# A planned order with other step lengths, one check instruction per unit pair, and a third PSUM bank for VectorE

## The chip, the core and the metric

The kernel runs on one core of a Trainium2 chip. The metric is the device time of one execution in microseconds. Five engines work side by side and meet through semaphores only: TensorE (PE) multiplies into PSUM, which has eight banks of 512 float32 per partition; ScalarE (ACT) and VectorE (DVE) read PSUM; GpSimd (POOL) works on SBUF; SyncE (SP) issues most DMAs. Each engine takes its own instructions strictly in the order in which they were written.

## The reference

Two branches over the same input `x` (2048 tokens of 512) are mixed by a gate.

```python
g = _sigmoid((x * gate_w).sum(-1, keepdims=True))
# A: 32 heads of 16, one shared key and value head
q = (x @ wq).reshape(B, S, H, Dh).transpose(0, 2, 1, 3)
k = x @ wk
v = x @ wv
scores = einsum('bhqd,bkd->bhqk', q, k) * Dh ** (-0.5)
p = softmax(scores, axis=-1)
a = einsum('bhqk,bkd->bhqd', p, v) ... @ wo
# B: gated MLP with a 2048 x 2048 mixing over tokens
z = gelu(einsum('bsd,df->bsf', x, w_in))
z1 = z[..., :Fh]
z2 = layernorm(z[..., Fh:])
g2 = einsum('ts,bsf->btf', w_sp, z2) + b_sp[None, :, None]
b = einsum('bsf,fd->bsd', z1 * g2, w_out)
return g * a + (1 - g) * b
```

The largest part is the exponential of the scores: 32 heads x 2048 queries x 2048 keys.

## The kernel before

**Blocks and units.** The scores are cut into blocks of 128 keys x 512 queries for one head. A unit is 512 queries and four heads, with 16 key tiles: 64 blocks. There are 32 units, so 2048 blocks. For each block PE forms scores (tile `ps` from `KA` and `QA`, "S" below), another engine forms the exponential, and PE multiplies it with the values ("PV").

**Two engines form the exponential.** ScalarE evaluates it directly for most blocks, two or three PSUM banks per instruction ("step", `exp_op`, L825), and writes tile `P`, a ring of `PB` slots of 512 columns. VectorE approximates it for the others by a polynomial of degree four: it reads the PSUM bank with a scale and an offset (`d_A`, L837, one bank or two neighbouring banks in one instruction), squares the result (`d_u`, L845) and squares it again (`d_w`, L851), all in tile `UW`. POOL can do part of the second squaring (also L851), in quarters of 256 columns; a block is two quarters. What the polynomial lacks in lower orders is added by small matmuls with `KTV` and `SVB`. VectorE gets its blocks in batches of four (one key tile, four heads); a batch reserves a slot of `UW`. No batch is fixed to an engine in advance: the planner opens a new batch when a VectorE bank comes free.

**Banks.** ScalarE's steps alternate between banks 0 and 1 and banks 2, 3 and 4 (`EB`). VectorE has bank 5 and may take bank 4 (`DBK`); when it does, ScalarE's step has two blocks in place of three. One bank collects PV (`BO`) and one serves all other matmuls (`BM`, the fill bank): projections, the gated MLP, the token mixing, the output rows. Those come as groups of matmuls that hold the bank from the first matmul until VectorE has read it. Where PE would be idle for too long, it gets a group of matmuls on zeros (tag "warm").

**The planner.** The order on every engine is written out before the launch by a discrete simulation inside the kernel file. Whichever engine has the earliest free time takes its next step (`pe_step`, `act_step`, `dve_step`, `pool_step`), with lengths from constants: one ScalarE step of n blocks keeps the engine for `426.7 * n + A_OV` ns (`act_period`); one VectorE read takes 601 ns and each further bank 533 ns; a square takes 65 ns plus 0.52 ns per column; a POOL square of n quarters takes `C_P0 + C_P1 * n`, 184 + 428 n. `C_SW` is the cost of changing between S and other matmuls on PE, `L_PE` and `L_X` the delays from one engine to another, `D_END` and `D_DEP` those behind a VectorE instruction. The hardware runs the resulting order; the constants matter there only through that order and through how many blocks went to each engine.

**Rules of the planner.** `hungry(now)` estimates VectorE's outstanding work, 600 ns for every PSUM bank that waits for it among it. Bank 4 goes to VectorE while `hungry` is below `FLEX`. A unit gives VectorE no more batches when fewer than `RMIN` (in the last unit `RLAST`) blocks would be left. `pool_try` starts POOL's work only for as long as VectorE is expected to read PSUM (`psum_work`), with a tolerance `PSL`: a POOL square of n quarters is issued if the coming reads last at least `C_P0 + C_P1 * n - PSL`.

**Checks and normalisation.** At the end of a unit VectorE transposes the PV bank to `T1`. After every second unit VectorE takes reciprocals (`rc`), POOL multiplies them with the gate (`rr`, L881) and applies them (`Tn`, L891). The polynomial is only good for bounded scores, so 16 units carry a check: POOL compares two columns of `T1` with a threshold (L916) and multiplies the outcome into `good` (L917). Two VectorE instructions reduce `good` to a flag near the end (`bad_ops`, L921 and L922); a flag other than zero would make all engines run a slow exact path.

Of the kernel before, what the change touches and what calls it, by code (L numbers as in the profile page):

```python
# [20 lines left out]
NST = 16  # L21
NU = 32
LN_EPS = 1e-5
PB = 24
ND = 6
NQ = 3
NMAX = 8
# [18 lines left out]
N0 = 3  # L46
A_OV = 63.3
HEAD = 45000.0
C_TN = 1250.0
C_T2 = 7000.0  # L50
# [120 lines left out]
def build_kernel(nc, x_d, wq_d, wk_d, wv_d, wo_d, win_d, wsp_d, bsp_d, wout_d, gw_d, out_d):  # L171
    es = ExitStack()
    with es:
# [62 lines left out]
        good = sb("good", [128, 16, 2], F32)  # L236
        gtmp = sb("gtmp", [128, 16, 2], F32)
# [28 lines left out]
        op("dve", lambda v: v.memset(good[:], 1.0), w=["good"])  # L266
# [136 lines left out]
        C_MM, C_V, C_344, C_SW, C_256, C_1ST = 216.0, 216.0, 146.0, 103.0, 110.0, 10.0  # L403
        L_PE, L_X = 250.0, 60.0
        D_END, D_DEP = 85.0, 117.0
        C_DA, C_TT, C_EV = 601.0, 1130.0, 600.0

        T = {}
# [502 lines left out]
            return lambda: pgx.op("dve", lambda v: v.transpose(OT.rearrange("p r b (g i) -> p r (b g i)", i=32)[:, c % 2, 512 * jp:512 * jp + 512], Tn[:, pr, :]),  # L911
                                  r=[("Tn", pr, 0, 0), ("Tn", pr, 1, 0)], w=[("OT", c % 2, jp)], tag="T2")

        def good_op(jj):
            def f():
                op("pool", lambda v: v.tensor_scalar(gtmp[:], t1v[:, jj, :, 17:19], thr[:, 0:1], None, ALU.is_le), r=[("T1", jj, 0), "thr"], w=["gtmp"], tag="good")  # L916
                op("pool", lambda v: v.tensor_tensor(good[:], good[:], gtmp[:], ALU.mult), r=["gtmp", "good"], w=["good"], tag="good")  # L917
            return f

        def bad_ops():  # L920
            op("dve", lambda v: v.tensor_reduce(goodp[:], good[:], AX.XY, ALU.min), r=["good"], w=["goodp"], tag="bad")  # L921
# [4 lines left out]
        def unit_end(u, t):  # L926
            c, j = u // 8, u % 8
            jj, jp = j % 2, j // 2
            pr = jp % 2
            if u == NU - 1:  # L930
                for h in range(2):
                    dq(t1_q, 370.0, t1_op(pg, u, 256 * h, 256 * h + 256), t, None)
                no = [norm_ops(pg, c, jp, [1], 8 * h, 8 * h + 8, [("T1", 1, 256 * h)]) for h in range(2)]
                for z in range(len(no[0])):
                    for h in range(2):
                        dq(t1_q, *no[h][z], t, None)
                for h in range(2):
                    rk = [("Tn", pr, 0, 0), ("Tn", pr, 1, 8 * h)]
                    dq(t1_q, 370.0, t2_op(pg, c, jp, 256 * h, 256 * h + 256, rk, ("OT", 3, 3, h)), t, setT(("OT", 3, 3, h)))
                return  # L940
            tf = t1_op(pg, u)

            def t1f():
                assert u < 2 or (u - 2) in t1_done, u
                tf()
            dq(t1_q, 625.0, t1f, t if u < 2 else (lambda: max(t, T.get(("TnE", (u - 2) // 2), 1e12))), setT(("O", u)))
            if chk_of(u) is not None:
                dq(pl_q, 390.0, good_op(jj), (lambda: when(("k2", 3), ("O", u))), None)
            if u == NU - 2:
                for c_, f_ in norm_ops(pg, c, jp, [0]):  # L950
                    dq(norm_q, c_, f_, (lambda: when("RT", ("O", u))), None)
                return
            if jj == 1:
                no = norm_ops(pg, c, jp, [0, 1], eng="pool", big=True)
                dq(norm_q, no[0][0], no[0][1], (lambda: when("RT", ("O", u))), setT(("rc", u)))
                dq(pl_q, 200.0, no[1][1], (lambda: when(("rc", u))), setT(("rr", u)))

                def tn():
                    no[2][1]()
                    t1_done.update((u - 1, u))  # L960
                def tne(t):
                    T[("TnE", u // 2)] = t
                    if jp == (2 if c == 3 else 3):
                        t2_dma(c, t)
                dq(pl_q, C_TN, tn, (lambda: when(("rr", u))), tne)
            if u == NU - 3:
                dq(norm_q, 250.0, bad_ops, (lambda: when(("TnE", u // 2))), setT("bad"))

        T["wqd0"] = 6400.0
        T["wqd"] = 17000.0  # L970
# [120 lines left out]
        def d_busy(b):  # L1091
            return b in slots and slots[b]["cur"] is not None

        def d_bank(now, flex=True):
            for b in DBK:
                d = dbs[b]
                if b < 5 and not flex:
                    continue
                if d["k"] is not None and (d["k"] not in eend or eend[d["k"]] + L_X > now):
                    continue  # L1100
                if d["blk"] is None and not d_busy(b) and max(d["free"], slots[b]["free"] if b in slots else 0.0) <= now:
                    return b
            return None
# [7 lines left out]
        def d_soon(now):  # L1111
            if d_busy(DBK[0]) or not (db["todo"] or new_batch(now)):
                return None
            t = []
            f = free["dve"]
            for b in DBK:
                if b < 5 and len(DBK) > 1:
# [118 lines left out]
        def add_checks(now):  # L1236
# [20 lines left out]
            if pu < NU and pu not in chk_added:  # L1257
# [3 lines left out]
                elif ("QS", q) in T:  # L1261
                    chk_added.add(pu)
                    for g in range(4):
# [2 lines left out]
                            T[("QSfree", q)] = clk["now"] + 300.0  # L1266
                        add_item(pu, g, (T[("QS", q)], f, None, None))

        def fill_pick(now):
            for b in slots:  # L1270
                s = slots[b]
                g = s["cur"]
                if g is not None and g.pos < len(g.pieces):
                    p = g.pieces[g.pos]
                    r = 0.0 if len(p) < 3 else p[2]()
                    if r is not None and r <= now:
                        return s, g, None
            cand = []
            if first:
                cand.append(first)  # L1280
            else:
                cand.append(early)
            if qs and 2 * qs[0][0] <= st_["ua"] + 3:
                cand.append(qs)
            cand += [outs, main, tails]
            for src in cand:
                if not src:
                    continue
                g = src[0][1] if src is qs else src[0]
                s = slots[g.bank]  # L1290
                if s["cur"] is not None or s["free"] > now:
                    continue
                r = g.ready()
                if r is not None and r <= now:
                    return s, g, src
            return None
# [21 lines left out]
        def pe_step(now):  # L1318
            r = pe_work(now)
            if r is None:  # L1320
# [8 lines left out]
                elif now > W_HEAD and b < (1.0 if now < 20000.0 else W_GEL if gst["arm"] and gst["t"] > now - 8000.0 else pr["W_MIN"]) * W_WIN:  # L1329
# [3 lines left out]
                    if (topen is None or t_end + 40.0 <= lim) and (ds is None or ds > t_end):  # L1333
                        zb = None
                        if (u < NU and all((u, g) in started for g in range(4)) and all(x < unit_total(u) // 4 for x in pv_g[u])
                                and slots[BO]["cur"] is None and slots[BO]["free"] <= now):
                            zb = BO
                        elif slots[BM]["cur"] is None and slots[BM]["free"] <= now:
# [331 lines left out]
        def pool_try(now, rem=0.0):  # L1670
# [27 lines left out]
            for m in sorted(pq):  # L1698
                hd, ud, wb, th, tu, pw = pq[m]
                i = 8 - pw  # L1700
                n = min(nh, i - wb)
                if n <= 0 or (i - 1) // 4 >= ud or tu + 80.0 > now:
                    continue
                d_w("pool", m, i - n, i, after=pg.ops["dve"][-2:-1])
                c_ = C_P0 + C_P1 * n
                plc["lock"] = now + c_
                plc["free"] = now + c_ + 60.0
                w_add(m, i - n, i, now + c_ + 100.0 + L_X)
                pq[m][5] = pw + n
                w_end(m)  # L1710
                return
# [14 lines left out]
        def dve_step(now):  # L1726
# [15 lines left out]
            rd = sorted((d["ord"], b) for b, d in dbs.items() if d["blk"] is not None and d["ready"] <= now)  # L1742
            if len(rd) == 1 and pr["HOLD"] and now > HEAD and st_["ua"] < NU - 1 and not gst["on"]:
                b = rd[0][1]
                o = dbs[DBK[1] if b == DBK[0] else DBK[0]]
# [257 lines left out]
```

## Time and profile before

| | us |
|---|---|
| median of 3 runs | 723.12 (723.04 to 724.63) |
| profiled execution | 723.15 |
| its span, first to last instruction | 721.3 |
| ScalarE busy | 704.6 |
| VectorE busy | 702.4 |
| PE busy | 700.9 |
| POOL busy | 519.7 |

The span is what the trace covers; 1.85 us of the profiled execution's time lie around it. PE's busy time says little about a limit, since its matmuls overlap and their ends are modelled. A row of a group of instructions gives the busy time of the group and the mean length of one, and a length includes the overlap with the instruction before it on the same engine, so lengths may add up to more than the engine's busy time.

### The profile page before, as it was taken

How to read it: one execution, taken by the hardware profiler on the slowest of the kernel's cores; microseconds unless marked ns; L12 is line 12 of the kernel's file. 1: busy time of each engine (PE TensorE's matmuls, PEld its weight loads, DVE VectorE, ACT ScalarE, POOL GpSimd, SP SyncE). 2: the span in 40 equal slices, each digit the busy share in tenths (PEclk: the TensorE clock that was granted, in tenths of full speed). 3: DMA queues.
4: the chain of work that ended last, by engine and by line, in shares of the span. 5: the costliest groups of instructions: out<-in, count | busy, mean ns of one | idle time of the engine just before them, and what ended most of it. 6: DMA issues, size and time to landing. Idle time of an engine off the chain costs nothing. (4 is left out here: it accounts for less than half of the span.)

```text
span 721.3 us, 20958 instructions
## 1 busy us (share of the span) xinstructions
PE 700.9 (97%) x8572; PEld 204.6 (28%) x8572; DVE 702.4 (97%) x1014; ACT 704.6 (98%) x759; POOL 519.7 (72%) x469
## 2 busy tenths in 40 slices
PE   8999999999999999999999999999999999999896
PEld 3322232234222232222223222222322222222222
DVE  5999999999999999999999999999999999999996
ACT  5999999999999999999999999999999999999995
POOL 5468778774467778787677877768877777777772
PEclk9999999999999999999999999999999999999999
DMA  8453000000001015000002410000150000000101
GB/s 162 130 99 64 2 1 2 2 2 3 2 1 31 2 30 97 24 1 2 1 2 39 102 39 9 2 2 1 31 90 16 16 16 17 1 2 2 31 2 34
DMA packets 59808, 20.07 MB, mean 28 GB/s; under 512 B 54805, under 2 KB 59193, under 8 KB 59705
## 3 DMA queue, kind: packets, MB, share of 16 engines
q1 hardware_dynamic: 57448, 18.36, 12.1%
q8 instruction: 69, 1.13, 0.7%
q10 hardware_dynamic: 2256, 0.30, 0.3%
q14 instruction: 35, 0.28, 0.1%
HBM read 3.38 MB, written 2.10 MB: 8 GB/s over the span
## 5 line engine op out<-in xcount | busy, mean ns | idle before, releaser
L825 ACT ACTIVATE P<-ps 128x1024 bf16<-128x1024 f32 (+1 forms) x739 | 679.4, 1211 | 1.8 <-PE ps L387 1.5
L851 POOL TENSOR_TENSOR UW<-UW 128x512 f16<-128x512 f16 (+2 forms) x331 | 426.6, 1289 | 144.0 <-DVE UW L851 59.8
L837 DVE TENSOR_SCALAR UW<-ps 128x512 f16<-128x512 f32 (+1 forms) x418 | 356.4, 874 | 3.2 <-PE ps L387 1.8
L387 PE MATMUL ps<-QA,KA 32*128 32x512 bf16 x2048 | 322.1, 384 | 11.6 <-ACT P L825 6.8
L387 PE MATMUL ps<-P,V 128*32 128x512 bf16 x1480 | 186.9, 386 | 0.2 <-DVE KN L558 0.2
L845 DVE TENSOR_TENSOR UW<-UW 128x2048 f16<-128x2048 f16 (+1 forms) x176 | 182.3, 1036 | 1.3
L387 PEld LDWEIGHTS ps<-QA,KA 32*128 32x128 bf16 x2048 | 88.8, 91 | 312.5 <-ACT P L825 162.9
L387 PE MATMUL ps<-wT,z 128*32 128x512 bf16 (+1 forms) x1536 | 113.4, 366 | 0.0
L387 PE MATMUL ps<-UW,V 128*32 128x512 f16 x568 | 109.6, 385 | 0.2
L851 DVE TENSOR_TENSOR UW<-UW 128x1024 f16<-128x1024 f16 (+5 forms) x161 | 99.4, 629 | 0.0
L387 PEld LDWEIGHTS ps<-P,V 128*32 128x32 bf16 x1480 | 42.6, 94 | 59.9 <-issue 57.6
L387 PEld LDWEIGHTS ps<-wT,z 128*32 128x32 bf16 x1536 | 26.4, 94 | 42.5 <-issue 42.2
L387 PE MATMUL ps<-wout,z 128*32 128x512 bf16 x384 | 32.5, 384 | 0.0
L534 POOL TENSOR_TENSOR QSQ<-QA 128x512 bf16<-128x512 bf16 x16 | 23.8, 1490 | 10.9 <-DVE QA L530 4.1
L387 PEld LDWEIGHTS ps<-UW,V 128*32 128x32 bf16 x568 | 25.4, 94 | 20.0 <-issue 14.8
L387 PE MATMUL ps<-win,xT 128*32 128x344 bf16 x512 | 30.3, 312 | 0.7 <-DVE z L641 0.4
L863 DVE STREAM_TRANSPOSE T<-ps 128x512 f32<-128x512 f32 (+1 forms) x33 | 22.8, 694 | 2.1 <-PE ps L387 2.1
L387 PE MATMUL ps<-CT,zer 128*32 128x512 bf16 x256 | 23.2, 382 | 0.0
L387 PE MATMUL ps<-CT,SVB 128*32 128x512 bf16 x128 | 22.8, 383 | 0.0
L387 PE MATMUL ps<-xT,win 128*32 128x512 bf16 (+1 forms) x384 | 22.3, 363 | 0.2 <-ACT P L825 0.2
L387 PE MATMUL ps<-QA,KTV 128*32 128x512 bf16 x128 | 22.3, 385 | 0.0
L387 PE MATMUL ps<-xT,wqd 128*32 128x512 bf16 x256 | 21.1, 384 | 0.3 <-DMA xT<-in_A_x_dram 0.2
(113 smaller groups left out, 326.1 us busy)
## 6 DMA issues: line engine op xcount, KB each, us to landing
out_dram<-outsb SPq DMA_DIRECT2D x15, 128.0 KB, 2.6
win<-in_B_w_in_dram SPq DMA_DIRECT2D x1, 1376.0 KB, 8.0
wout<-in_B_w_out_dram SPq DMA_DIRECT2D x1, 640.0 KB, 4.6
wo<-in_A_wo_dram SPq DMA_DIRECT2D x8, 64.0 KB, 2.3
KA<-KA SPq DMA_DIRECT2D x4, 112.0 KB, 2.4
UW<-in_A_wq_dram SPq DMA_DIRECT2D x1, 384.0 KB, 4.0
wT<-in_B_w_sp_dram SPq DMA_TRANSPOSE x16, 4.5
UW<-in_A_wq_dram ACTq DMA_DIRECT2D x1, 128.0 KB, 4.1
```

What stands on the lines that cost most here:

```text
L387: return t.matmul(dst, lhsT, rhs, start=start, stop=stop, tile_position=tp)
L534: dq(pl_q, 1050.0, lambda: op("pool", lambda v: v.tensor_tensor(QSQ[:, q % 2, :], QA[:, q % NQ, :], QA[:, q % NQ, :], ALU.mult), r=[("Q", ...
L825: op("act", lambda a: a.activation(P[:, 512 * p0:512 * (p0 + n)], ps[:, 512 * b0:512 * (b0 + n)], ACT.Exp), r=[bkey(b0 + i_) for i_ in ran ...
L837: op("dve", lambda v: v.tensor_scalar(UW[:, s, 512 * i:512 * (i + n)], bank(b, 512 * n), Q_A, Q_AS, ALU.mult, ALU.add), r=[bkey(b + j) for ...
L845: op("dve", lambda v: v.tensor_tensor(src, src, src, ALU.mult), r=k, w=k, tag="dTT")
L851: op(eng, lambda v: v.tensor_tensor(src, src, src, ALU.mult), r=[("U", s, h) for h in range(a // 2, (b + 1) // 2)], w=w, after=after, tag= ...
L863: return lambda: pgx.op("dve", lambda v: v.transpose(T1[:, jj, c0:c1], bank(BO, c1 - c0, c0)), r=[bkey(BO)], w=[("T1", jj, c0)], tag="T1")
```

## The change

It changes the planner's constants and some of its rules, the check, and which banks VectorE may use. The work of the reference, its matmuls and its DMAs stay as they are; the order of all of them is planned anew.

- VectorE's banks are 5, 6 and 4. The fill bank is bank 6 now (it was 7) and the PV bank is 7. VectorE gets bank 6 only when no fill group holds it, when `hungry` is below `BMH` and when the fill work is not behind a straight line that ends at `TFE` (`lag`). Fill groups wait while VectorE has the bank.
- A check is one POOL instruction that writes a slot of its own in `good`; the multiplication into a common tile and the memset of it go. The reduction at the end covers 512 columns in place of 32.
- The ring `P` has 26 slots in place of 24.
- The lengths that the planner assumes: `A_OV` 63.3 to 50, `C_SW` 103 to 98, `L_X` 60 to 40, `D_DEP` 117 to 105; a check 390 to 370, `rr` 200 to 260, the reduction 250 to 750; the normalisation of the last but one unit now counts POOL's hold of the port. Quarters that POOL squares count as ready 400 ns later (`PMG`).
- Thresholds: `RLAST` 12 to 20, `RMIN` 36 to 44, `FLEX` 5000 to 3500, `D_HG` 2800 to 2600, `PSL` 80 to 0, `TTR` 0 to 50 and others.

```diff
-PB = 24
+PB = 26
-DBK = (5, 4)
-BKO = 6
+DBK = (5, 6, 4)
+SHB = 4
+BKO = 7
-RLAST = 12
+RLAST = 20
-A_OV = 63.3
+A_OV = 50
-PR = dict(HALF=100.0, IDR=10, IDN=4, WRES=16, D_HG=2800.0, D_FL=False, WIN=1000.0, WIH=560.0, BACK=32, PRESS=5, FLEX=5000.0, RMIN=36, WBL=0.5, W_MIN=0.8, TTR=0.0, PMX=3, WMX=1000.0, PTO=6000.0, PSL=80.0, WP0=45000.0, WG=0, HOLD=0.0, RLEND=0)
+PR = dict(HALF=50.0, IDR=11, IDN=4, WRES=18, D_HG=2600.0, D_FL=False, WIN=1000.0, WIH=560.0, BACK=34, PRESS=5, FLEX=3500.0, RMIN=44, WBL=0.4, W_MIN=0.78, TTR=50.0, PMX=3, WMX=1000.0, PTO=6000.0, PSL=0.0, WP0=45000.0, WG=0, HOLD=0.0, RLEND=0, BMH=2400.0, FST=0.0, TFE=760000.0, PMG=400.0)
+NCHK = 16
+L_PE = 250
+L_X = 40
+D_END = 85
+D_DEP = 105
+C_SW = 98
...
-        def good_op(jj):
-            def f():
-                op("pool", lambda v: v.tensor_scalar(gtmp[:], t1v[:, jj, :, 17:19], thr[:, 0:1], None, ALU.is_le), r=[("T1", jj, 0), "thr"], w=["gtmp"], tag="good")
-                op("pool", lambda v: v.tensor_tensor(good[:], good[:], gtmp[:], ALU.mult), r=["gtmp", "good"], w=["good"], tag="good")
-            return f
+        def good_op(jj, i):
+            return lambda: op("pool", lambda v: v.tensor_scalar(good[:, i, :, :], t1v[:, jj, :, 17:19], thr[:, 0:1], None, ALU.is_le),
+                              r=[("T1", jj, 0), "thr"], w=[("good", i)], tag="good")
...
+        def d_bm(now):
+            if now < HEAD or hungry(now) >= pr["BMH"] or gst["arm"] and (gel or gst["on"]):
+                return False
+            return not lag(now)
...
+        def lag(now):
+            if gst["arm"] and (gel or gst["on"]):
+                return True
+            n = sum(len(g.pieces) for q in (early, main, outs) for g in q)
+            if ft["n"] is None:
+                ft["n"] = n
+                ft["t"] = now
+            return n > ft["n"] * (pr["TFE"] - now) / (pr["TFE"] - ft["t"])
...
-                if b < 5 and not flex:
+                if b == SHB and not flex or b == BM and not d_bm(now):
...
-                if s["cur"] is not None or s["free"] > now:
+                if s["cur"] is not None or s["free"] > now or g.bank in dbs and (dbs[g.bank]["blk"] is not None or dbs[g.bank]["free"] > now):
...
-                w_add(m, i - n, i, now + c_ + 100.0 + L_X)
+                w_add(m, i - n, i, now + c_ + 100.0 + L_X + pr["PMG"])
```

More of the change, by code (lines that the diff above doesn't have):

```diff
@@ L235, in build_kernel @@
         thr = sb("thr", [128, 1], F32)
-        good = sb("good", [128, 16, 2], F32)
-        gtmp = sb("gtmp", [128, 16, 2], F32)
+        good = sb("good", [128, NCHK, 16, 2], B16)
         goodp = sb("goodp", [128, 1], F32)
@@ L401, in build_kernel @@
             mm(bank(0), CT[:, 0:128], CT[:], True, True, ["CT"], [bkey(0)], tag="warm")
-        C_MM, C_V, C_344, C_SW, C_256, C_1ST = 216.0, 216.0, 146.0, 103.0, 110.0, 10.0
-        L_PE, L_X = 250.0, 60.0
-        D_END, D_DEP = 85.0, 117.0
+        C_MM, C_V, C_344, C_256, C_1ST = 216.0, 216.0, 146.0, 110.0, 10.0
         C_DA, C_TT, C_EV = 601.0, 1130.0, 600.0
@@ L966, in unit_end @@
             if u == NU - 3:
-                dq(norm_q, 250.0, bad_ops, (lambda: when(("TnE", u // 2))), setT("bad"))
+                dq(norm_q, 750.0, bad_ops, (lambda: when(("TnE", u // 2))), setT("bad"))
         T["wqd0"] = 6400.0
@@ L1116, in d_soon @@
             for b in DBK:
-                if b < 5 and len(DBK) > 1:
+                if b in (SHB, BM):
                     continue
@@ L1290, in fill_pick @@
                 s = slots[g.bank]
-                if s["cur"] is not None or s["free"] > now:
+                if s["cur"] is not None or s["free"] > now or g.bank in dbs and (dbs[g.bank]["blk"] is not None or dbs[g.bank]["free"] > now):
+                    continue
+                if g.bank == BM and now > HEAD and not first and src is not qs and hungry(now) < pr["FST"] and not lag(now):
                     continue
@@ L1337, in pe_step @@
                             zb = BO
-                        elif slots[BM]["cur"] is None and slots[BM]["free"] <= now:
+                        elif slots[BM]["cur"] is None and slots[BM]["free"] <= now and dbs[BM]["blk"] is None and dbs[BM]["free"] <= now:
                             zb = BM
```

14 lines of the change are left out of this document (7 added, 7 removed).

## The prediction

> **What bounds the kernel now.** I read the page first (span, busy times), then the busy time by stretches of the span, cut where ScalarE's first and last exponentials and its gelu stage stand, then the groups of instructions with shapes kept apart.
>
> ```profile
> span 721.3 us, 20958 instructions
> PE 700.9 (97%) x8572; PEld 204.6 (28%) x8572; DVE 702.4 (97%) x1014; ACT 704.6 (98%) x759; POOL 519.7 (72%) x469
> ...
> core 0: us, PE busy (x) PEld busy (x) DVE busy (x) ACT busy (x) POOL busy (x), PEclk, DMA share, GB/s
> 0.00:9.01 9.01, 7.34 (x111) 3.19 (x115) 4.31 (x15) 1.56 (x2) 5.00 (x24) 1.00 0.90 164
> 9.01:155.25 146.24, 140.04 (x1966) 44.87 (x1952) 141.06 (x207) 145.46 (x159) 107.08 (x104) 1.00 0.21 47
> 155.25:178.15 22.90, 22.69 (x411) 10.66 (x407) 22.83 (x64) 22.40 (x16) 11.66 (x14) 1.00 0.01 3
> 178.15:712.19 534.04, 527.51 (x6074) 144.57 (x6062) 530.37 (x719) 533.94 (x582) 395.95 (x328) 1.00 0.10 21
> 712.19:721.30 9.11, 3.33 (x56) 1.33 (x54) 3.81 (x12) 1.26 (x2) 0.00 (x0) 0.90 0.21 67
> ```
>
> In the long stretch from 178.15 to 712.19 ScalarE is busy for 533.94 of 534.04 us and VectorE for 530.37. Before it, from 9.01 to 155.25, ScalarE lacks 0.78 us. So the exponentials leave ScalarE with 0.9 us of idle time to win back, and VectorE with hardly more. Head (9.0) and end (9.1) are the only stretches where both stand still, and the diff leaves their work as it is. PE is no third bound: its waits are mostly for the other two to release a bank.
>
> ```profile
> PEld ps L387 <- ACT P L825: 163.7, 384, 1.2
> PEld ps L387 <- DVE UW L837: 85.8, 219, 0.9
> ```
>
> These two (us in total, times, longest) say that PE stood ready 384 times before ScalarE had read its bank, and 219 times before VectorE had. The time can therefore fall only if ScalarE gets less work, and with VectorE full that means VectorE's work must get cheaper, or ScalarE's own blocks.
>
> ```profile
> L825 ACT ACTIVATE P<-ps 128x1024 bf16<-128x1024 f32 x735 | 674.9, 1211 | 0.8 <-PE ps L387 0.6
> L825 ACT ACTIVATE P<-ps 128x1536 bf16<-128x1536 f32 x3 | 4.4, 1453 | 0.9 <-PE ps L387 0.9
> L387 PE MATMUL ps<-P,V 128*32 128x512 bf16 x1480 | 186.9, 386 | 0.2 <-DVE KN L558 0.2
> L387 PE MATMUL ps<-UW,V 128*32 128x512 f16 x568 | 109.6, 385 | 0.2
> ```
>
> The value matmuls count the blocks: 1480 came from ScalarE and 568, that is 142 batches of four, from VectorE. A two-block step takes 674.9/735 = 0.918 us, a block 0.459, a batch on ScalarE 1.84.
>
> ```profile
> L837 DVE TENSOR_SCALAR UW<-ps 128x1024 f16<-128x1024 f32 x150 | 182.2, 1215 | 2.1 <-PE ps L387 1.7
> L837 DVE TENSOR_SCALAR UW<-ps 128x512 f16<-128x512 f32 x268 | 174.2, 683 | 1.1 <-PE ps L387 0.2
> L845 DVE TENSOR_TENSOR UW<-UW 128x2048 f16<-128x2048 f16 (+1 forms) x176 | 182.3, 1036 | 1.3
> L851 DVE TENSOR_TENSOR UW<-UW 128x1024 f16<-128x1024 f16 (+5 forms) x161 | 99.4, 629 | 0.0
> ...
> 300.59 1.29 DVE L837 TENSOR_SCALAR UW<-ps 128x512 f16<-128x512 f32 x2
> 301.80 1.21 DVE L845 TENSOR_TENSOR UW<-UW 128x2048 f16<-128x2048 f16 x1
> ...
> 703.88 1.20 DVE L837 TENSOR_SCALAR UW<-ps 128x1024 f16<-128x1024 f32 x1
> 705.01 0.67 DVE L851 TENSOR_TENSOR UW<-UW 128x1024 f16<-128x1024 f16 x1
> 705.61 0.67 DVE L845 TENSOR_TENSOR UW<-UW 128x1024 f16<-128x1024 f16 x1
> 706.21 1.20 DVE L837 TENSOR_SCALAR UW<-ps 128x1024 f16<-128x1024 f32 x1
> ```
>
> Lengths overlap, so I take starts from the timeline. A read of two banks lasts 705.01 - 703.88 = 1.13 us, two single reads 301.80 - 300.59 = 1.21, or 0.60 each, and a square of 1024 columns 0.60, or 0.15 for a quarter. All batches then cost 150 x 1.13 + 268 x 0.60 for the reads, and 281.7 less 337 overlaps of 0.07 for the squares: 588 us, 4.14 a batch. This gives the **exchange rate**. If VectorE gains X us, the two engines end together again once X/(4.14 + 1.84) batches have moved, and the end comes 1.84/5.98 = 0.31 X sooner. If ScalarE gains Y, the end comes 0.69 Y sooner. Everything below is turned into time with these two rates.
>
> **The change, part by part.**
>
> *ScalarE's step* (`A_OV`). The constant 63.3 makes a two-block step 853.4 + 63.3 = 916.7 ns, and the trace has 918. The new one makes it 903.4. The hardware will not follow, so over some 735 steps the plan runs 9.8 us ahead of ScalarE. In the plan both engines end together 0.69 x 9.8 = 6.8 us earlier, which takes 6.8/4.14 = 1.6 batches from VectorE; on the chip these 6.6 blocks fall to ScalarE: **+3.0 us**. What speaks for the shorter step is that PE then offers scores early and waits for ScalarE, not the reverse; the 0.9 us above may vanish: 0.69 x 0.9, **-0.6**. Bounds for the two together are -0.6 and +3.0; I take both in full, +2.4, since I see no row by which a plan with shorter steps gives VectorE as many batches. The shorter `C_SW`, `L_X` and `D_DEP` shorten waits of the plan that the trace no longer has as idle time: 0.
>
> [...]
>
> *Third bank, pairs.* Banks 4, 5 and 6 are neighbours, so two reads in line become one more often. Each new pair saves 1.21 - 1.13 = 0.08 us by the starts, 0.07 with 0.60 a read. There are 268 single reads, so at most 134 pairs: 0 to 9.4 us. I take 100, 7.0 us, since 300 of 568 blocks are in pairs with two banks already: **-2.1**.
>
> *Third bank, three-block steps.* When VectorE's blocks fit into 5 and 6, or wait there so that `hungry` passes the new 3500, bank 4 stays with ScalarE. With the planner's 426.7 per block, which the 918 bears out, 65 ns of a step are fixed; a third block in a step saves 65/2 = 32 ns. The only three-block steps in the trace, in the head, took 4.4/3 = 1.47 us against 1.38 for one and a half pairs, but PE was late there (0.9 idle); so the bounds are 90 ns lost and 32 won for each. The number may lie between 0 and some 300, every second step at most. I take 80, the smaller side, because the old limit of 5000 let only 3 through and the new one is not far under it: 2.6 us of ScalarE, **-1.8**.
>
> *POOL's part of the squares.*
>
> ```profile
> L851 POOL TENSOR_TENSOR UW<-UW 128x512 f16<-128x512 f16 x165 | 247.9, 1502 | 84.2 <-DVE UW L851 39.8 <-DVE UW L837 25.4 <-DVE z L641 4.6
> L851 POOL TENSOR_TENSOR UW<-UW 128x256 f16<-128x256 f16 x129 | 103.9, 805 | 38.6 <-DVE UW L851 15.5 <-DVE UW L837 9.4 <-DVE UW L845 1.2
> L851 POOL TENSOR_TENSOR UW<-UW 128x768 f16<-128x768 f16 x37 | 74.9, 2024 | 21.1 <-DVE UW L845 8.2 <-DVE UW L837 6.4 <-DVE UW L851 4.4
> L917 POOL TENSOR_TENSOR good<-good,gtmp 128x32 f32<-128x32 f32 x16 | 7.1, 442 | 1.3
> L916 POOL TENSOR_SCALAR gtmp<-T,thr 128x32 f32<-128x32 f32 x16 | 7.0, 440 | 2.7 <-POOL UW L851 1.5 <-DVE T L863 0.4 <-DVE UW L837 0.3
> ```
>
> POOL does 129 + 2 x 165 + 3 x 37 = 570 of 1136 quarters, and stands idle for 144 us before them, so it has time, but is let in only while VectorE reads PSUM. With `PSL` at 0 one quarter (612 planned) no longer fits beside one single read (601); two (1040) fit beside a pair (1134), three (1468) beside a pair and a single. Ends: all 129 one-quarter squares go back to VectorE, 129 x 0.15 = 19.4 us, +6.0; or the 144 us fill at 426.7/570 = 0.75 a quarter, 192 quarters, 28.8 us, -8.9. With longer reads I take 30 quarters more, 4.5 us: **-1.4**. The 400 ns that `PMG` adds delay only when PV may use a quarter; the next batch's blocks are its cover, and with that gone PE would wait, which costs ScalarE nothing until its own scores stand behind it.
>
> *Checks.* 16 instructions of L917 go: 7.1 + 1.3 = 8.4 us of POOL, 11 quarters at 0.75, 1.7 us of VectorE; the shorter hold of POOL's port may save 0.8 more. At worst nobody uses the time, at best every instruction held up a square and 7.1 us come back (-2.2). I take 2.5 us: **-0.8**. The wider reduction comes once:
>
> ```profile
> L921 DVE TENSOR_REDUCE goodp<-good x1: 173/173/173, 679.5 to 679.5; 128x1 f32<-128x32 f32 x1
> L512 DVE TENSOR_REDUCE km<-ps 128x1 f32<-128x512 f32 x4 | 2.7, 674 | 0.0
> ```
>
> From 173 to about 674 ns, the row of another reduction of 512 columns: 0.5 us, **+0.2**. It waits for all 16 slots, as the old one waited for all 16 multiplications.
>
> *The wait that is added.* A fill group must now wait until VectorE has read bank 6, 0.6 to 1.13 us and what stands before it. PE is in order, so behind that group's first matmul stand the next scores of both engines. The plan starts a group only when the bank is free by its own clock, so this costs only where the chip lags the plan: 0 on ScalarE while PE has the slack of its 384 waits. `RLAST` and `RMIN` move a batch or so at unit ends, at most 1.84 us either way: 0. No DMA is added or changed; their issue follows the plan.
>
> Sum: +3.0 - 0.6 - 2.1 - 1.8 - 1.4 - 0.8 + 0.2 = -3.5 us. The profiled execution took 723.15 (span 721.3 and 1.85 around it), the median is 723.12, so the two hardly differ: **719.6 us**.
>
> **The rivals.**
>
> *No change.* VectorE was never short of banks: before all its reads it waited 1.9 us for PE (1.7 and 0.2 in the two rows). A third bank then only shuffles work, or is hardly lent, since fill groups hold it. The pairs, steps, quarters and checks bring half (-3.1), the step length costs what it costs (+2.4) and the reduction 0.2: -0.5, 722.6. For it speak the two rates: 10 us saved on VectorE are 3 in the end.
>
> *Slower.* POOL loses its one-quarter squares to the 11 ns between 601 and 612. Each lost quarter costs 0.15 x 0.31 = 0.046 us. With the other terms as summed, but the three-block steps and checks at half and no quarters gained, the rest stands at +2.4 - 2.1 - 0.9 - 0.4 + 0.2 = -0.8; it becomes clearly slower from (2.2 + 0.8)/0.046 = 65 quarters lost, and with all 129 it is +5.2: 728.3. Against it speaks that reads come in pairs more often.
>
> *Much faster.* ScalarE keeps bank 4 in most even steps, 300 three-block steps: 300 x 0.032 x 0.69 = -6.6 in place of -1.8: 714.8. Against it: VectorE's blocks are then confined to 5 and a shared 6.
>
> **How the numbers follow.** About 0.3%, 2.2 us, is what a measurement of this kernel can tell from no change. Forecast 0.40, much faster 0.12, no change 0.30, slower 0.18. The first two are faster by more than that: 0.52; same 0.30; slower 0.18. The bounds of the single terms add up to far more on both sides, but do not fall together. The range reaches from a little under the much faster case, 714, to 726, which leaves out most of the slower case and a little below.
>
> **What would show it.** The count of value matmuls from `UW`: 568 or more if VectorE gained, some 560 if the step length took its batches. Reads of 1024 columns on L837: about 250 in place of 150. Three-block steps: about 80. POOL quarters: about 600; under 510 the slower case. L917 gone. ScalarE's step still 0.918, and its idle time under 1 us; if VectorE shows idle time for PE of 5 us or more, the plan ran ahead of the chip. I would be wrong above all if the shorter step length moved more to ScalarE than 7 blocks, or if many three-block steps came.

## The result, and the profile after

The changed kernel takes 727.47 us (median of 20 executions, 723.04 to 733.54) against 723.09 before: a ratio of 1.0065 with a 95% interval of 1.0044 to 1.0087. Forecast were 719.6 and a range of 714 to 726, so both the sign and the range were wrong. The executions of the kernel before lie within about 2 us of each other; those of the changed kernel spread over 10.5 us. One execution of the kernel before (1067.55 us) and one of the last run below (941.15 us at a granted clock of 0.557) lie far outside all others and are left out of the ratios and the spreads.

The first thing to see is what goes with that spread. Each execution has a mean granted clock of PE:

```
granted clock   us
0.998           723.04  723.78
0.997           724.24
0.994 to 0.995  725.23  726.10  726.20  726.27  726.30  726.82
0.987 to 0.989  727.45  727.49  728.08  728.36  728.40  729.83
0.979 to 0.982  731.20  731.63  732.42  732.68  733.54
```

A straight line through the 20 points is 723.0 + 474 x (1 - clock) us and leaves 0.5 us of scatter. At full clock the changed kernel is as fast as the one before; the whole loss goes with the clock. That the clock is the cause and not only a companion is tested below.

The profiled execution is one with a clock of 0.994 and took 726.20 us. Its page, first the span, the busy times and the row of the granted clock in 40 slices (tenths):

```profile
span 724.2 us, 20754 instructions
PE 697.8 (96%) x8512; PEld 204.7 (28%) x8512; DVE 699.2 (97%) x992; ACT 706.4 (98%) x757; POOL 495.0 (68%) x422
PEclk9999999999999999999999999998999999999999
```

One slice shows an 8. The busy time by stretches around it (length; busy us and count for PE, weight loads, VectorE, ScalarE, POOL; granted clock; DMA), cut at the edges that the trace gives for the lower clock, 500.86 and 507.69 us, and in steps of 3.41 us from there:

```profile
490.62:494.03 3.41, 3.41 (x44) 0.98 (x40) 3.41 (x4) 3.41 (x5) 3.06 (x3) 1.00 0.00 0
494.03:497.45 3.42, 3.42 (x42) 0.86 (x45) 3.28 (x5) 3.42 (x5) 3.13 (x3) 1.00 0.00 0
497.45:500.86 3.41, 2.58 (x25) 0.57 (x23) 3.41 (x6) 3.41 (x5) 2.85 (x4) 1.00 0.00 0
500.86:507.69 6.83, 6.83 (x53) 1.11 (x51) 4.16 (x7) 5.00 (x6) 1.58 (x2) 0.50 0.01 2
507.69:511.10 3.41, 3.41 (x44) 0.86 (x40) 3.04 (x5) 3.38 (x4) 2.48 (x2) 1.00 0.00 0
```

For 6.83 us PE has half its clock. In that stretch ScalarE is busy for 5.00 us and VectorE for 4.16: both wait for scores. Between 34 us and its last step, the gelu stage apart, ScalarE loses more than 0.04 us at no other place. Just ahead lie 3.41 us in which PE issued 25 matmuls, where its neighbours have 42 and 44, although ScalarE and VectorE were busy throughout. The timeline of PE and its weight loads there, with the wait in brackets, shows what PE did:

```profile
497.99 0.11 PEld L392 LDWEIGHTS ps<-QA,KA 32*128 32x128 bf16 x5 [0.48 <-ACT P L828]
497.99 0.60 PE L392 MATMUL ps<-QA,KA 32*128 32x512 bf16 x5
498.90 0.09 PEld L392 LDWEIGHTS ps<-QA,KA 32*128 32x128 bf16 x2 [0.81 <-ACT P L828]
498.91 0.39 PE L392 MATMUL ps<-QA,KA 32*128 32x512 bf16 x2 [0.32 <-ACT P L828]
...
499.82 0.11 PEld L392 LDWEIGHTS ps<-QA,KA 32*128 32x128 bf16 x3 [0.49 <-ACT P L828]
499.83 0.60 PE L392 MATMUL ps<-QA,KA 32*128 32x512 bf16 x3 [0.20 <-ACT P L828]
500.74 0.09 PEld L392 LDWEIGHTS ps<-QA,KA 32*128 32x128 bf16 x2 [0.81 <-ACT P L828]
500.74 0.53 PE L392 MATMUL ps<-QA,KA 32*128 32x512 bf16 x2 [0.31 <-ACT P L828]
```

Twice PE goes from scores straight to the next scores (at the dots lie four value matmuls), and each of the three times it stands until ScalarE has read its bank. The five scores at 497.99 are two for ScalarE and three for VectorE, into banks 5, 6 and 4 by the order that the kernel wrote: VectorE holds the fill bank, so no fill group can start. A group of zeros could have gone to the PV bank, into which 188 of this kernel's 196 matmuls on zeros go by the same order; the plan put none here, and no run shows why (a run below adds four groups in this place, all in the PV bank). What follows is the loss of the clock.

The groups that the prediction's terms rest on are these after the change:

```profile
L828 ACT ACTIVATE P<-ps 128x1024 bf16<-128x1024 f32 x721 | 664.5, 1224 | 2.1 <-PE ps L392 2.1
L828 ACT ACTIVATE P<-ps 128x1536 bf16<-128x1536 f32 x13 | 20.1, 1549 | 1.8 <-PE ps L392 1.7
L392 PE MATMUL ps<-UW,V 128*32 128x512 f16 x564 | 104.9, 385 | 0.0
L840 DVE TENSOR_SCALAR UW<-ps 128x1024 f16<-128x1024 f32 x148 | 180.1, 1217 | 1.9 <-PE ps L392 1.4
L840 DVE TENSOR_SCALAR UW<-ps 128x512 f16<-128x512 f32 x268 | 174.8, 683 | 5.4 <-PE ps L392 3.8
L854 POOL TENSOR_TENSOR UW<-UW 128x512 f16<-128x512 f16 x152 | 226.1, 1488 | 92.8 <-DVE UW L854 43.3 <-DVE UW L840 27.3 <-DVE z L668 8.5
L854 POOL TENSOR_TENSOR UW<-UW 128x768 f16<-128x768 f16 x48 | 97.2, 2025 | 28.5 <-DVE UW L840 11.5 <-DVE UW L854 9.6 <-DVE UW L848 4.9
L854 POOL TENSOR_TENSOR UW<-UW 128x256 f16<-128x256 f16 x100 | 80.7, 807 | 28.7 <-DVE UW L840 7.5 <-DVE UW L848 6.0 <-DVE UW L854 1.7
L392 PE MATMUL ps<-CT,zer 128*32 128x512 bf16 x196 | 14.8, 382 | 0.0
```

VectorE has 564 blocks, one batch fewer. Pairs of banks are read 148 times (150 before), single banks 268 times as before: the third bank made no pairs. Three-block steps went from 3 to 13. POOL squares 100 + 2 x 152 + 3 x 48 = 548 quarters (570 before). The matmuls on zeros fell from 256 to 196, that is from 64 groups of four to 49. By the order that the kernel writes, bank 6 gets 33 of the 564 blocks.

### The profile page after: what moved, and what is told of

Read it like the earlier page. It is cut to its first block, busy times and chain, and to the rows that moved or that the text cites. A ratio compares the mean times of both kernels' runs of the same rounds, so it can differ in the third digit from the quotient of the medians.

```text
span 724.2 us, 20754 instructions
## 1 busy us (share of the span) xinstructions
PE 697.8 (96%) x8512; PEld 204.7 (28%) x8512; DVE 699.2 (97%) x992; ACT 706.4 (98%) x757; POOL 495.0 (68%) x422
## 4 chain that ended last, share of the span: by engine, by line
PE 49%; ACT 14%; issue 3%; DVE 3%; ACTq 0%; DVEq 0%
PE ps L392 49%; ACT P L828 14%; DVE UW L840 2%; DVE UW L848 0%; DVE UW L854 0%; DVE win L894 0%; DVE T L866 0%; DVE rc L884 0%; DVE z L745 0%; ACT outsb L786 0%; DVE QA L533 0%; ACTq L166 0%; DVE z L712 0%; DVE rc L879 0%; DVE win L910 0%
## 5 line engine op out<-in xcount | busy, mean ns | idle before, releaser
L854 POOL TENSOR_TENSOR UW<-UW 128x512 f16<-128x512 f16 (+2 forms) x300 | 404.1, 1347 | 150.0 <-DVE UW L854 54.6
L840 DVE TENSOR_SCALAR UW<-ps 128x512 f16<-128x512 f32 (+1 forms) x416 | 353.8, 873 | 7.2 <-PE ps L392 5.2
L848 DVE TENSOR_TENSOR UW<-UW 128x2048 f16<-128x2048 f16 (+1 forms) x160 | 177.3, 1109 | 0.8
L392 PEld LDWEIGHTS ps<-QA,KA 32*128 32x128 bf16 x2048 | 86.7, 91 | 318.5 <-ACT P L828 176.6
L392 PE MATMUL ps<-UW,V 128*32 128x512 f16 x564 | 104.9, 385 | 0.0
L392 PE MATMUL ps<-wout,z 128*32 128x512 bf16 x384 | 31.0, 384 | 0.0
L392 PEld LDWEIGHTS ps<-UW,V 128*32 128x32 bf16 x564 | 23.8, 94 | 17.5 <-issue 13.6
L392 PE MATMUL ps<-QA,KTV 128*32 128x512 bf16 x128 | 24.5, 384 | 0.0
L894 POOL TENSOR_TENSOR win<-T,rc 128x512 bf16<-128x512 f32 x11 | 18.1, 1641 | 9.4 <-DVE UW L854 6.2
```

Source lines behind the costliest of these rows:

```text
L392: return t.matmul(dst, lhsT, rhs, start=start, stop=stop, tile_position=tp)
L840: op("dve", lambda v: v.tensor_scalar(UW[:, s, 512 * i:512 * (i + n)], bank(b, 512 * n), Q_A, Q_AS, ALU.mult, ALU.add), r=[bkey(b + j) for ...
L848: op("dve", lambda v: v.tensor_tensor(src, src, src, ALU.mult), r=k, w=k, tag="dTT")
L854: op(eng, lambda v: v.tensor_tensor(src, src, src, ALU.mult), r=[("U", s, h) for h in range(a // 2, (b + 1) // 2)], w=w, after=after, tag= ...
L894: pgx.op(eng, lambda v: v.tensor_tensor(dst, t1v[:, j0:j1, b0:b1, 0:16], rc[:, j0:j1, b0:b1].unsqueeze(3).broadcast_to([128, n, nb, 16]), ...
```

## The experiments

Two readings are used in all runs. The granted clock is the mean over an execution; about 0.999 is what an execution without a low stretch has, since its very end is low (from 719.53 us on in the profile of before, from 722.73 us on in that of the changed kernel). ScalarE's **waits** are summed from the trace over all of its steps but the one behind the gelu stage: the time from one step's end to the next one's end, less 0.42667 us per block and 0.0633 us per step, which is the pace at which its steps end in both kernels wherever PE is early (0.917 us for two blocks). Before it had 1.8 us of waits; the changed kernel has 3.1, of which 2.4 lie in the one low stretch. In the first four runs two theories beside the clock were open: that the split of blocks between the engines cost the time, and that the lent bank did.

### The old step length alone

```diff
-A_OV = 50
+A_OV = 63.3
```

> The changed kernel with the old length of a ScalarE step (63.3 in place of 50), the rest as changed; the order is planned anew. Clock theory: the time above 723.0 comes from stretches of 6.8 us at half the PE clock, some 2.3 us each, which arise where PE runs ahead of ScalarE by the plan and then has too little to multiply. With the true length PE does not run ahead: mean granted clock 0.998 in nearly all executions, spread under 2 us, median 721 to 723. Split theory: the loss is the batch that went to ScalarE (564 blocks on VectorE in place of 568); then 568 again and 1.8 us less than 727.5, about 725.7, with the spread of 10 us still there. Bank theory: the loss comes from bank 6 being lent; then nothing changes, 727.

727.56 us (727.22 to 728.42), ratio 1.0065 (1.0052 to 1.0079), clock 0.996 to 0.999, 568 blocks on VectorE. The clock came back and the spread went, as the clock theory had it, but the time did not fall at all: none of the three theories foresaw that. A steady loss of 4 us stood in the place of the unsteady one. ScalarE's waits are 6.9 us, spread over the whole run, and the group of its steps shows where they hide:

```profile
L828 ACT ACTIVATE P<-ps 128x1024 bf16<-128x1024 f32 x715 | 661.8, 1086 | 2.4 <-PE ps L392 1.7
```

The idle time (2.4 us) is small, but a step's mean length is 1086 ns against 1211 before. A step that is issued early overlaps the one before it and so looks long; one whose scores come late looks short: in the profile of the changed kernel the steps at 502.89, 504.37 and 505.91 us, with 0.37 to 0.52 us of waiting for PE ahead of them, are 1.02 us long, against a mean of 1.22. Here PE is late more often, and it costs without showing as idle time.

### The new step length alone

```diff
 # in the kernel before
-A_OV = 63.3
+A_OV = 50
```

> The kernel before with the new length alone (50 in place of 63.3). Clock theory: it gets the same stretches at half clock: granted clock 0.98 to 0.995, median 725 to 729, spread of several us. Split theory: 140 batches are planned in place of 142, 3.7 us more on ScalarE less what VectorE's waits hid: 725 to 727, but a steady time and a clock of 0.999. Bank theory: 723 to 724, no different from before.

729.62 us (727.92 to 730.27), ratio 1.0081 (1.0068 to 1.0095); 560 blocks on VectorE. The clock is 0.995 to 0.999, so low stretches do come (one of 3.4 us in the profile), but fewer than in the changed kernel, and at 0.999 the time is still 727.9. Most of this loss is the split: two batches more on ScalarE, 3.7 us at 1.84 each. Each theory held in part, and neither forecast (725 to 729 and 725 to 727) reaches the time.

### More matmuls on zeros

```diff
-PR = dict(..., W_MIN=0.78, ...)
+PR = dict(..., W_MIN=0.85, ...)
```

> The changed kernel with more matmuls on zeros (planned where PE would multiply less than 85% of a window in place of 78%: 86 groups of four in place of 49). Clock theory: fewer stretches at half clock: mean granted clock above 0.995 in most executions, median 723 to 725, spread halved. Split theory: still 141 batches, so 727. Bank theory: 727.

724.91 us (724.01 to 726.41), ratio 1.0021 (1.0012 to 1.0030), clock 0.995 to 1.0, still 564 blocks on VectorE. The clock theory foresaw 723 to 725 and a clock above 0.995; the split theory 727. The order is planned anew here, with 86 groups of zeros in place of 49, and at a clock of 0.998 and more it takes 724.0 to 725.4 us, more than the 723.0 to 723.8 of the changed kernel. So a test in an unchanged order follows below.

### The old limit for zeros alone

```diff
-PR = dict(..., W_MIN=0.78, ...)
+PR = dict(..., W_MIN=0.8, ...)
```

> The changed kernel with the old limit for matmuls on zeros alone (80% of a window in place of 78; 59 groups in place of 49). If the lowered limit is what cost the clock: clock 0.997, 723.5 to 725. If the limit is measured in the plan's time, which runs 1.5% ahead of ScalarE, and the fill bank is away, two points hardly matter: 725.5 to 728, clock 0.985 to 0.995.

724.75 us (723.48 to 726.17), ratio 1.0017 (1.0009 to 1.0026), clock 0.996 to 1.0. The first of the two forecasts was right: two points of that limit, ten groups of zeros in an order planned anew, are worth 2.7 us here. The three executions at 0.998 and above took 723.5 to 723.7.

### Bank 6 not lent

```diff
         def d_bm(now):
+            return False
```

> The changed kernel without lending bank 6 to VectorE (the fill bank stays with the fill groups), the rest as changed; planned anew, 140 batches. Clock theory: the stretches at half clock stay, since the step length stays: clock 0.98 to 0.995, median 726 to 730. Bank theory: they go, 723. Split theory: one batch less on VectorE: 729, steady.

725.11 us (724.87 to 727.09), ratio 1.0036 (1.0024 to 1.0047), 560 blocks, clock mostly 0.999. None of the three times that were forecast came. That most of the low stretches are gone speaks for the bank theory and against the step length alone being enough; but this plan also has 55 groups of zeros in place of 49, so the bank isn't shown to be the cause by itself. The time at full clock, 725.0, is 2 us above that of the changed kernel, because a batch went back to ScalarE. So the lent bank gives a batch and, as far as this run tells, takes clock.

### The changed order, with zeros where PE waited

```diff
+        def zeros():
+            ...   # at 15 places one or two groups of matmuls on zeros; no time passes in the plan
         def s_mm(dst_bank, blk, key):
+            zeros()
```

> The changed kernel in its own order on every engine, with nothing planned anew; at 13 places, where PE waited 0.23 us or more for ScalarE or VectorE in the trace, one or two groups of four matmuls on zeros are put in front of the scores. Clock theory: the time above 723 goes with the stretches at half clock: mean granted clock 0.997 to 0.999, median 723 to 724.5, spread under 3 us. Split theory (the loss lies in the blocks and in ScalarE's waits, and the clock only follows): no gain, 727, or worse for the added work.

724.32 us (723.16 to 728.53), ratio 1.0017 (1.0004 to 1.0030). Eight of the eleven executions have a clock of 0.997 or more and took 723.2 to 725.3; the median is as the clock theory forecast, the spread of under 3 us is missed by one execution with 728.5 at 0.989. This is the cleanest test, since the blocks and the order of all other work on every engine are those of the changed kernel and PE has 25 groups more to do, 24 of them in the PV bank. ScalarE's waits fall from 3.1 to 1.8 us. In the timeline of PE at the same place the gaps are filled and the clock stays:

```profile
498.68 0.60 PE L392 MATMUL ps<-QA,KA 32*128 32x512 bf16 x5
499.21 0.62 PE L392 MATMUL ps<-CT,zer 128*32 128x512 bf16 x8
499.76 0.39 PE L392 MATMUL ps<-QA,KA 32*128 32x512 bf16 x2
...
500.51 0.60 PE L392 MATMUL ps<-QA,KA 32*128 32x512 bf16 x3
501.05 0.62 PE L392 MATMUL ps<-CT,zer 128*32 128x512 bf16 x8
501.59 0.39 PE L392 MATMUL ps<-QA,KA 32*128 32x512 bf16 x2
```

One low stretch is left in its profile, near 42 us, where no zeros had been added.

### The order before, without its zeros

```diff
 # in the kernel before
-                            for g in range(4):
-                                mm(ps[32 * g:32 * g + 32, 512 * zb:512 * zb + 512], zer[:, 32 * g:32 * g + 32], CT[:], ...)
```

> The kernel before in its own order, without the matmuls on zeros that its plan put into idle time of PE from 20 us on to the last unit. Nothing else depends on them. Clock theory: stretches at half clock appear, each 2 to 2.5 us: clock 0.97 to 0.99, median 727 to 735 with a spread of several us. Split theory: same blocks, same waits, less work on PE: 723.

735.57 us (731.80 to 739.94), ratio 1.0159 (1.0129 to 1.0189), clock 0.950 to 0.969. Taking away work that computes nothing cost 12 us, a little more than forecast. The stretches of the profile around one of the low ones look as in the changed kernel: 25 and 22 matmuls in 3.4 us each, then half the clock.

```profile
538.40:541.80 3.40, 3.03 (x25) 0.95 (x21) 3.40 (x5) 3.40 (x5) 2.09 (x2) 1.00 0.86 136
541.80:545.20 3.40, 2.82 (x22) 0.86 (x21) 3.37 (x5) 3.40 (x5) 3.02 (x2) 1.00 0.00 0
545.20:558.90 13.70, 13.41 (x98) 2.18 (x94) 9.62 (x14) 9.82 (x11) 6.64 (x7) 0.50 0.00 1
```

### The second check instruction put back

```diff
+                op("pool", lambda v: v.tensor_scalar(gtmp[:], ...), w=["gtmp"])
+                op("pool", lambda v: v.tensor_tensor(good[:, i, :, :], gtmp[:], gtmp[:], ALU.mult), w=[("good", i)])
```

> The changed kernel in its own order, with the second POOL instruction of each of the 16 checks put back (a product into the check's own slot). Prices the check alone: by the prediction 0.8 us slower than the changed kernel (bounds 0 and 2.2), as far as the clock lets it be seen: compare executions of the same granted clock. If POOL is never waited for, 0.

727.25 us (725.57 to 728.73), ratio to before 1.0053 (1.0039 to 1.0067). At a clock of 0.994 it took 726.4, the changed kernel 726.1 to 726.8; at 0.989 it took 728.1, the changed kernel 727.5 to 728.4. In this order the second instruction costs nothing that can be seen.

### All old lengths

```diff
-A_OV = 50
+A_OV = 63.3
-L_X = 40
+L_X = 60
-D_DEP = 105
+D_DEP = 117
-C_SW = 98
+C_SW = 103
```

> The changed kernel with the old lengths of ScalarE's step, of the delays between engines (60), behind a VectorE instruction (117) and of PE's change of kind (103); the thresholds, the third bank and the check as changed; planned anew, 142 batches. The changed kernel with the old step length alone had 568 blocks on VectorE and no stretch at half clock, yet 727.6, with 6.9 us in which ScalarE's exponentials ended later than its own pace. Theory A: those waits come from the shorter delays, which the short ScalarE step hides by letting PE run ahead; then they fall under 3 us here and the time is 721 to 723.5. Theory B: they come from the third bank and the thresholds (more single reads, 334 against 268); then they stay, 726 to 728.

723.09 us (722.34 to 725.53), ratio 1.0005 (0.9996 to 1.0014). Theory A: ScalarE's waits fall from 6.9 to 2.5 us and the loss is gone, although single reads are nearly as many (312) as in the run with 727.6 (334). So with the right step length the three shorter constants (`L_X`, `D_DEP`, `C_SW`; none was tried alone) made PE late, and the short step length hid it in the changed kernel by letting PE run ahead. One rival is not separated: this plan also has fewer groups of zeros, 56 against 96 in the run with 727.6. Against it speaks that the run with 86 groups has only 2.4 us of waits.

### All old lengths, bank 6 not lent

The four lengths of the run above, and `return False` in `d_bm`.

> All old lengths, thresholds and check as changed, but bank 6 not lent. Planned anew, 141 batches in place of 142. Prices the third bank where the plan's lengths are right. If the bank is worth the batch that it brings: 1.8 to 3 us slower than the run with it (723.1), 725 to 726, clock 0.998. If it only takes work from the fill bank and with it from PE: the same or faster, 722 to 723.

723.67 us (723.20 to 724.05), ratio 1.0005 (0.9996 to 1.0014), clock 0.998 to 1.0 in all eleven executions, 564 blocks. The executions at 0.999 and above took 723.2 to 724.1 (median 723.4), with the bank lent 722.3 to 723.1 (722.8). So where the lengths are right the bank is worth about 0.7 us at full clock, less than the 1.8 to 3 us forecast in case its batch counted, and without it no execution shows a low stretch, with 62 groups of zeros against 56: its batch saves 1.8 us of steps, but ScalarE's waits are 0.8 us without it and 2.5 with it.

### Looking for an order that beats both

Two steps. First two new plans:

```diff
 # all old lengths, W_MIN=0.8, PMG=0.0                    (143 batches)
 # all old lengths but A_OV = 57, W_MIN=0.85              (142 batches)
```

> All old lengths as in the run that took 723.1, the old limit for matmuls on zeros (80% of a window), and POOL's quarters counted as ready without the added 400 ns; third bank, check and the other thresholds as changed. Planned anew: 143 batches on VectorE, one more than before. If blocks on ScalarE and waits add up as in the other runs: head 9, steps 675.8, gelu stage 23.7, end 9, waits 2.5, around 1.9: 721.9, so a little faster than before (723.2). If the earlier quarters make PE wait for POOL and ScalarE for PE, the waits pass 5 us: 724 or more.

> All old lengths but a ScalarE step of 57 in place of 63.3, matmuls on zeros up to 85% of a window, the rest as changed; 142 batches, 70 groups of zeros. A step a little short should keep ScalarE's waits under 2 us, and the zeros the clock: 721.5 to 723. If the short step alone lowers the clock again: 724 to 727 and a clock under 0.995.

722.28 us (721.24 to 726.46), ratio 0.9998 (0.9984 to 1.0011), and 721.87 us (721.19 to 725.22), ratio 0.9991 (0.9979 to 1.0002). Each has executions at 0.988 to 0.992 with 724.5 us or more, so neither is clear of before. Then zeros were added to these two orders in their low windows, with nothing planned anew:

> The order of the run with a step length of 57, with 6 groups of four matmuls on zeros added at places where PE waited in its low windows (around 78, 146 to 152 and 674 us). That run took 721.2 to 722.6 in executions with a clock of 0.996 or more and 724.5 to 725.2 at 0.992. If the clock is all that spread it: 721.2 to 722.3 in nearly all executions, median 721.6, clear of before (723.2). If not: the 725 stay.

> The order of the run with 143 batches, with 23 groups of four matmuls on zeros added where PE waited in low windows. It took 721.2 to 722.8 at a clock of 0.998 and more, 724.6 to 726.5 below 0.992. If the clock is all: median 722.0, nothing above 723.5. If the zeros stand in the way of scores: 722.5 to 723.5 at full clock.

The first took 721.41 us (720.75 to 722.02), ratio 0.9973 (0.9962 to 0.9983); the second 721.74 us, ratio 0.9983 (0.9974 to 0.9992). The clock is 0.998 or 0.999 in every execution of both. Six groups of zeros removed the 725s of the first. Two of its stretches, cut at the edges of the kernel before, can be laid beside those in the prediction, though its gelu stage comes later (167.3 to 188.8 us) and lies partly in the second: ScalarE is busy for 532.32 of 532.85 us there, and its waits are 0.5 us in all.

```profile
9.01:155.25 146.24, 140.86 (x1977) 45.97 (x1970) 139.94 (x214) 145.72 (x156) 104.58 (x101) 1.00 0.20 46
...
178.15:711.00 532.85, 527.90 (x6216) 149.62 (x6208) 529.22 (x753) 532.32 (x571) 384.76 (x300) 1.00 0.10 21
```

## Why the prediction was wrong

**The step that failed** is the reading of PE: "PE is no third bound: its waits are mostly for the other two to release a bank", and what followed from it, that an earlier PE is pure gain ("PE then offers scores early and waits for ScalarE, not the reverse") and that the lent bank costs "0 on ScalarE while PE has the slack of its 384 waits". PE's slack isn't free. In the profile above it was busy for 2.58 us, with 25 matmuls, in 3.41 us; the loss of half its clock followed, and for 6.83 us it was the bound. The page of before had no low slice between head and end, and I did not ask what kept it so: 64 groups of matmuls on zeros, whose row I had and did not price.

```profile
PEclk9999999999999999999999999999999999999999
L387 PE MATMUL ps<-CT,zer 128*32 128x512 bf16 x256 | 23.2, 382 | 0.0
```

The run without them prices them at 12 us. The change cut them to 49, kept fill groups from their bank by lending it, and sent PE ahead of ScalarE. Undoing any one of the three (old limit 724.8, no lending 725.1, old lengths 723.1) brings most of the clock back. Each of these plans also has some more groups of zeros (59, 55 and 56 against 49), so they don't say what each of the three is worth; that the clock is the cause and no companion is shown by the zeros added to an unchanged order (724.3).

**The terms of the sum**, at full clock, where the changed kernel is level with before. There ScalarE has four blocks more and two steps fewer, +1.6 us at its pace, and 1.1 us less of waits; that makes +0.5, and the two executions at 0.998 show 0 to 0.7.

- *Step length, +3.0.* Direction right, size too large: one batch was lost (564 blocks), 1.8 us, not 1.6 batches and 3.0 us. In the kernel before the new length alone took two batches.
- *Waits that vanish, -0.6.* Right as far as it went: outside the low stretch the changed kernel has 0.7 us of waits, against 1.8 before. But it bought more than that, because of the next point.
- *Shorter delays, 0.* Wrong, and hidden: without the short step they cost 4.5 us (727.6 against 723.1, both planned anew, with the rival named there). I argued that the trace had no idle time left to shorten; the point was that PE could become late.
- *Pairs, -2.1.* Nothing: 148 pairs in place of 250. Bank 6 takes 33 blocks. I counted neighbouring banks and not how often the fill bank is free.
- *Three-block steps, -1.8.* Mis-sized: 13, not 80, so about -0.3 by the same 32 ns each.
- *POOL's quarters, -1.4.* Wrong sign: 548 after 570 before, not 600.
- *Checks, -0.8.* Nothing that can be seen, at the end of the range given. The 0.8 us for POOL's hold that went into it was an estimate without a row. Single holds do stand in the profile of before: a square of 1024 columns on VectorE begins at 257.68 us, 0.39 us before a square on POOL ends, and the next square begins 0.86 us after it, against the 0.60 that the prediction took.
- *The reduction, +0.2.* Not measured by itself.

One reading of the rows was off too, though no term uses it: VectorE had not "hardly more" idle time than ScalarE's 0.9 us, but 8.9 (146.24 less 141.06 and 534.04 less 530.37).

**The rivals.** "No change" is what the kernel does at full clock, and for the reason given there: the bank is hardly lent. The slower rival came true in its sign but not in its mechanism; POOL lost quarters, but 22, not 65. Of the signs I named, VectorE's 5 us of waiting for PE did appear (L840, 1.4 + 3.8), but more than half of it is a trace of the half clock: 3.0 us lie ahead of four reads in that stretch and just behind it.

How often the low stretches come differs from one execution to the next, though order and work are the same: the 20 executions of the changed kernel have clocks from 0.979 to 0.998. What sets that was not tried, and no run shows it. PE has the same order in the run with the second check instruction, but its profile has three low stretches in place of one, at 41.58, 502.38 and 550.17 us, and a clock of 0.989 against 0.994.

## What to carry to other kernels

Idle time of PE can have a price that the waits of one profile don't show; here the kernel before took 735.57 us without its matmuls on zeros and 723.1 with them. Before a change shortens PE's work or lets it run ahead, look for the stretches in which it does least (here 25 matmuls in 3.41 us, where the two stretches before had 44 and 42), and look at the granted clock of many executions, not of the profiled one. Constants of a planner that are each a little wrong can cover for each other; put them right together, or test each against the others. And a resource that is lent (here the fill bank) should be counted by how often it is free, not by what it could do.

## What the runs showed of the hardware

- Stretches at half clock between head and end lasted, for example, 3.4 us (the kernel before with the new step length alone), 6.83 us (the changed kernel) and 13.7 us (the kernel before without its zeros). In the profile of the changed kernel full clock is first recorded at 5.93 us; the clock is then full for 494.933 us, half for 6.827 and full again for 215.040. In the profile of before it is full for 713.386 us from 6.14 us on. In these two profiles the four lengths are 145, 2, 63 and 209 times 3.41333 us, the 63rd part of 215.040, each to within 0.001 us. What sets them was not tried, and no run shows it.
- PE did not stand idle ahead of the loss: in the 3.41 us before it, it was busy for 2.58 us with 25 matmuls of 512 columns, against 3.42 us with 42 and 3.41 us with 44 in the two stretches before.
- Neither the number of matmuls nor PE's busy time in such a stretch decides alone. 25 matmuls are followed by half clock in the changed kernel (497.45 to 500.86 us), and by full clock in the kernel before without its zeros (538.40 to 541.80 us). 2.82 us of busy time are followed by half clock in the latter (541.80 to 545.20 us), and 2.76 us by full clock in the kernel before (74.41 to 77.82 us). What exactly counts stays open.
- A stretch of 6.83 us costs about 2.2 us of the kernel's time by an estimate from the line above: 474 us times 0.0047, the clock's share that it takes (half of 6.83 in 724). ScalarE's waits in and just behind that stretch add up to 2.4 us.
- A ScalarE that is fed late need not show idle time: with 6.9 us of waits the trace showed 2.4 us idle in front of its two-block steps, and the rest only as shorter steps (1086 ns against 1211).
